# A fused linear-attention and expert kernel: the opening's loads reordered, three tiles transposed on TensorE, and the norm issued two tiles ahead

## The chip, the cores and the metric

The kernel runs on one core of one Trainium2 chip. The metric is the device time of one launch in microseconds, as the median of repeated runs. A core has five engines that work side by side and meet through semaphores: TensorE (PE in the profile, with weight loads shown apart as PEld), VectorE (DVE), ScalarE (ACT), GpSimd (POOL) and SyncE (SP), which only issues transfers. Each engine executes its instructions strictly in the order in which the program gives them.

## The reference

A sequence of 2048 tokens with 640 columns is normalised, and the sum of three things is returned: the input, a linear attention over the normalised input, and an expert layer that adds its own input and changes eight tokens of it.

```python
xn = layernorm(x)                                  # over 640 columns
# A: linear attention, 32 heads of 20 columns
q, k, v = split(xn @ wqkv)
phi = lambda t: where(t > 0, t + 1, exp(t)) + 1e-6
kv = einsum("bhsd,bhse->bhde", phi(k), v)
z = einsum("bhsd->bhd", phi(k))
o = einsum("bhqd,bhde->bhqe", phi(q), kv) / (einsum("bhqd,bhd->bhq", phi(q), z)[..., None] + 1e-6)
A = o @ wo
# B: one expert for the 8 tokens with the largest r
r = xn @ w_r
idx = argsort(-r)[:8]
y = (silu(xn[idx] @ w_gate) * (xn[idx] @ w_up)) @ w_down * sigmoid(r[idx])
B = xn, with y added to the rows idx
return x + A + B
```

## The kernel before

The tokens are cut into 16 tiles of 128. All of x, its normalised form `xn`, the transposed `xnT`, phi of q (transposed, `pqT`) and phi of k (`pk`) stay in SBUF.

**The main loop** (lines 365 to 398) takes one tile per iteration. TensorE makes k of the tile (`k_mm`, line 240, ten products, whose last column is the router's r), then a part of the product of `xn` and `pk` of the tile before (`ga_mm`, line 263, three products; `pk` of the tile before is its operand), then q (`q_mm`, line 252, 25 products with the weights `wq` as the stationary operand). ScalarE makes exp and relu of k and q (`phi_act`, lines 220 and 223) and copies the router column to `r_all` (line 384). VectorE joins exp and relu to `pk` and `pqT` (`phi_vec`, line 232).

**The layer norm** of a tile is made ahead of the loop's use of it. `ln_stats` runs two statistics instructions (line 161) and joins them (line 165) on VectorE; then come four small steps on columns of one element: add epsilon (169), a power for the root (174), a second power for the reciprocal (176), and a copy of the mean (177). They run on GpSimd, apart from the first tiles (those below `LN_FAST`), where VectorE copies the mean and takes the reciprocal. `ln_norm` (line 189) then writes `xn` on VectorE. From tile `PE_TR` on a DMA transpose, issued by SP (line 194), writes `xnT`; the tiles below are transposed on TensorE (`tr_tile`, line 199) and copied from PSUM (`tr_evict`).

The order on each engine is that of the program text (the tile framework is in manual schedule). In iteration t VectorE does: the statistics of tile t + 4, `pqT` of tile t - 1, the norm of tile t + 3, `pk` of tile t; from iteration 12 also residual additions (line 354). Small constants on GpSimd (`small_consts`) and the later loads on SP (`late_loads`, line 337) follow at the end of an iteration.

**The opening** (lines 100 to 111) issues the first loads from two queues, SP and ACT: x tile 0 in two halves, the k weights `wk` on ACT in two parts around x tiles 1 and 2 on SP, then the q weights `wq` and x tile 3 on SP, and x tiles 4 to 7 on ACT. Meanwhile TensorE runs `WARM` = 13 products of zeros (line 273). The router weights `wrow` are transposed by TensorE and copied into the last column of `wk` (line 284).

**After the loop** come the choice of the eight tokens, the sums over the tokens, the expert, the denominators, the per-head products, and an output loop (line 689) over the 16 tiles.

Of the kernel before, what the change touches and what calls it, by code (L numbers as in the profile page):

```python
# [8 lines left out]
P = 128  # L9
S = 2048  # L10
D = 640
# [3 lines left out]
T = S // P  # L15
KC = D // P
FC = F // P
C = 8
TBLK = 512
# [4 lines left out]
EB = 80  # L24
NEB = D // EB
EPS_BF16 = 1.0013580322265625e-05
PE_TR = 2
LN_FAST = 3
WARM = 13
LASTW = 448  # L30
AHEAD = 4

BF16 = mybir.dt.bfloat16
# [10 lines left out]
def kernel(  # L44
# [13 lines left out]
    nc = tc.nc  # L58
# [4 lines left out]
    x_v = A_x[0].rearrange("(t p) d -> p t d", p=P)  # L63
    out_v = out[0].rearrange("(t p) d -> p t d", p=P)
    wqkv_v = A_wqkv.rearrange("(kc p) n -> p kc n", p=P)
# [6 lines left out]
    def sb(shape, dt, name, tag=None):  # L72
        return big.tile(shape, dt, tag=tag or name, name=name)

    def pair(tag, name):
        return psum.tile([P, 2 * TBLK], F32, tag=tag, name=name)

    def bank(tag, name):
        return psum.tile([P, TBLK], F32, tag=tag, name=name)

    x_sb = sb([P, T, D], BF16, "x_sb")
    xn = sb([P, T, D], BF16, "xn")
    xnT = sb([P, KC, S], BF16, "xnT")
    pqT = sb([P, KC, S], BF16, "pqT")
    pk = sb([P, T, D], BF16, "pk")
    wk = sb([P, KC, D + 1], BF16, "wk")
    wq = sb([P, KC, D], BF16, "wq")
    wv = sb([P, KC, D], BF16, "wv")
# [12 lines left out]
    nc.gpsimd.dma_start(wrow[:], B_w_r.rearrange("(kc p) -> kc p", p=P))  # L101
    nc.sync.dma_start(x_sb[:, 0, 0:HW], x_v[:, 0, 0:HW])
    nc.scalar.dma_start(x_sb[:, 0, HW:D], x_v[:, 0, HW:D])
    nc.scalar.dma_start(wk[:, 0:2, 0:D], wqkv_v[:, 0:2, D : 2 * D])
    for t in (1, 2):
        nc.sync.dma_start(x_sb[:, t, :], x_v[:, t, :])
    nc.scalar.dma_start(wk[:, 2:KC, 0:D], wqkv_v[:, 2:KC, D : 2 * D])
    nc.sync.dma_start(wq[:, 0:3, :], wqkv_v[:, 0:3, 0:D])
    nc.sync.dma_start(wq[:, 3:KC, :], wqkv_v[:, 3:KC, 0:D])
    nc.sync.dma_start(x_sb[:, 3, :], x_v[:, 3, :])  # L110
    nc.scalar.dma_start(x_sb[:, 4:8, :], x_v[:, 4:8, :])


    zero = sb([P, TBLK], BF16, "zero")
# [43 lines left out]
    def ln_half(t, h):  # L158
        if h == 0:
            stat[t] = work.tile([P, 2, nc.vector.BN_STATS_DIM], F32, tag="stats", name=f"st{t}")  # L160
        nc.vector.bn_stats(out=stat[t][:, h, :], in_=x_sb[:, t, h * HW : (h + 1) * HW])  # L161

    def ln_aggr(t):
        mv = work.tile([P, 2], BF16, tag="mv", name=f"mv{t}", bufs=4)
        nc.vector.bn_aggr(out=mv[:], in_=stat[t][:])  # L165
        sc = work.tile([P, 2], F32, tag="sc", name=f"sc{t}", bufs=4)
        sq = work.tile([P, 2], BF16, tag="sq", name=f"sq{t}", bufs=4)
        scal[t] = sc, sq
        (nc.vector if t == 0 else nc.gpsimd).tensor_scalar(  # L169
            out=sq[:, 0:1], in0=mv[:, 1:2], scalar1=EPS_BF16, scalar2=None, op0=ALU.add  # L170
        )
        if t < LN_FAST:
            nc.vector.tensor_copy(sc[:, 0:1], mv[:, 0:1])  # L173
        nc.gpsimd.tensor_tensor(out=sq[:, 1:2], in0=sq[:, 0:1], in1=half[:], op=ALU.pow)  # L174
        if t >= LN_FAST:
            nc.gpsimd.tensor_tensor(out=sc[:, 1:2], in0=sq[:, 1:2], in1=neg1[:], op=ALU.pow)  # L176
            nc.gpsimd.tensor_copy(sc[:, 0:1], mv[:, 0:1])  # L177

    def ln_stats(t):
        ln_half(t, 0)  # L180
        ln_half(t, 1)
        ln_aggr(t)

    def ln_norm(t):
        sc, sq = scal[t]
        if t < LN_FAST:
            nc.vector.reciprocal(sc[:, 1:2], sq[:, 1:2])
        for a, b in ((0, 2 * P), (2 * P, D)) if t == 0 else ((0, D),):
            nc.vector.tensor_scalar(  # L189
                out=xn[:, t, a:b], in0=x_sb[:, t, a:b], scalar1=sc[:, 0:1], scalar2=sc[:, 1:2],  # L190
                op0=ALU.subtract, op1=ALU.mult,
            )
        if t >= PE_TR:
            nc.sync.dma_start_transpose(xnT[:, :, t * P : (t + 1) * P], xn[:, t, :])

    def tr_tile(t):
        ptr = bank("D1", f"tr{t}").bitcast(BF16)
        for kc in range(KC):
            nc.tensor.transpose(
                ptr[:, kc * P : (kc + 1) * P], xn[:, t, kc * P : (kc + 1) * P], ident[:]  # L200
            )
        return ptr

    def tr_evict(t, ptr):
        src = ptr[:, 0:D].rearrange("p (k f) -> p k f", k=KC)
        dst = xnT[:, :, t * P : (t + 1) * P]
        if t == 0:
            nc.scalar.copy(dst[:, 0:2, :], src[:, 0:2, :])
            nc.scalar.copy(dst[:, 2:KC, :], src[:, 2:KC, :])
        elif t == 1:  # L210
            nc.vector.tensor_copy(dst, src)
        else:
            nc.scalar.copy(dst, src)

    r_all = sb([P, T], BF16, "r_all")

# [18 lines left out]

    def k_mm(t):
        ps = pair("A", f"k{t}")
        for kc in range(KC):
            for a, b in ((0, TBLK), (TBLK, D + 1)):
                nc.tensor.matmul(  # L240
                    ps[:, a:b],
                    lhsT=xnT[:, kc, t * P : (t + 1) * P],
                    rhs=wk[:, kc, a:b],
                    start=(kc == 0), stop=(kc == KC - 1),
                )
        return ps

    def q_mm(t):
        ps = pair("B", f"q{t}")
        for m in range(KC):  # L250
            for kc in range(KC):
                nc.tensor.matmul(  # L252
                    ps[:, m * P : (m + 1) * P],
                    lhsT=wq[:, kc, m::KC],
                    rhs=xnT[:, kc, t * P : (t + 1) * P],
                    start=(kc == 0 and m in (0, 4)), stop=(kc == KC - 1),
                    skip_group_check=True,
                )
        return ps
# [11 lines left out]
    warm = pair("B", "warm")  # L271
    for i in range(WARM):
        nc.tensor.matmul(warm[:, 0:TBLK], lhsT=zero[:, 0:P], rhs=zero[:], start=True, stop=True)
# [4 lines left out]
    pg = bank("D0", "pg").bitcast(BF16)  # L278
    nc.tensor.transpose(pg[:, 0:P], headg[:].rearrange("p j h -> p (j h)"), ident[:])
    nc.scalar.copy(grep[:], pg[:, 0:P])  # L280
    tr_evict(0, tr_tile(0))
    prep = bank("D0", "prep").bitcast(BF16)
    nc.tensor.transpose(prep[:, 0:KC], wrow[:], ident[0:KC, 0:KC])
    nc.scalar.copy(wk[:, :, D], prep[:, 0:KC])  # L284
    ln_stats(1)
    ln_stats(2)
    ln_norm(1)
    ln_stats(3)

    iof = sb([P, 32], F32, "iof")  # L290
    boff = sb([NTB, 1], F32, "boff")
# [43 lines left out]
    def late_loads(t):  # L335
        def part(dst, src, a, b):
            nc.sync.dma_start(dst[:, a:b, :], src[:, a:b, :])

        wv_v = wqkv_v[:, :, 2 * D : 3 * D]
        plan = {  # L340
            0: (x_sb, x_v, 8, 12), 1: (wv, wv_v, 0, 3), 2: (wv, wv_v, 3, KC),
            3: (x_sb, x_v, 12, 16), 4: (wo, wo_v, 0, 4), 5: (wo, wo_v, 4, 8),
            6: (wg, kcF, 0, 2), 7: (wg, kcF, 2, 4), 8: (wg, kcF, 4, 5),
            9: (wu, kcU, 0, 2), 10: (wu, kcU, 2, 4), 11: (wu, kcU, 4, 5),
            12: (wd, kcD, 0, 6), 13: (wd, kcD, 6, 12),
        }
        if t in plan:
            part(*plan[t])
# [15 lines left out]

    for t in range(T):
        kp = k_mm(t)
        if t == 0:
            tr_evict(1, tr_tile(1))
        else:
            ga_mm(t - 1)  # L370
        qp = q_mm(t)
        if t == 0:
            ln_norm(2)
        else:
            if t == 1:
                q_phi(t - 1, qer)
            if t + 4 < T:
                ln_stats(t + 4)
            if t > 1:
                q_phi(t - 1, qer)  # L380
            if t + 3 < T:
                ln_norm(t + 3)
        ker = phi_act(kp, "k")
        nc.scalar.copy(r_all[:, t : t + 1], kp[:, D : D + 1])
        if t > 12:
            residual(4 * (t - 13) + 3)
        phi_vec(pk[:, t, :], ker, False)
        if t == 0:
            ln_norm(3)
            ln_stats(4)  # L390
        qer = phi_act(qp, "q")
        if t > 11:
            for u in range(4 * (t - 12), 4 * (t - 12) + 3):
                residual(u)
        small_consts(t)
        late_loads(t)
        if t > 12:
            keep(4 * (t - 13), 4 * (t - 12))
# [31 lines left out]
    for t in range(T):  # L430
        i = t % 4
        for a, b in ((0, TBLK), (TBLK, D)):
            nc.tensor.matmul(
                zp[32 * i : 32 * i + 32, a:b],
                lhsT=ones_bf[:],
                rhs=pk[:, t, a:b],
                start=(t < 4), stop=(t >= T - 4),
# [23 lines left out]
    for t in range(6):  # L461
# [4 lines left out]
        start=True, stop=True,  # L466
# [59 lines left out]
    for m in range(KC):  # L526
        for j in range(NTB):
            nc.tensor.matmul(  # L528
                pden[32 * j : 32 * j + 32, :],
                lhsT=zm[:, m, :],  # L530
                rhs=pqT[:, m, j * TBLK : (j + 1) * TBLK],
                start=(m == 0), stop=(m == KC - 1),
# [12 lines left out]
    for a, w in enumerate((wg, wu)):  # L545
        for kc in range(KC):
            for j in range(4):
                nc.tensor.matmul(  # L548
                    gu[32 * j : 32 * j + 32, a * TBLK : a * TBLK + FJ],
                    lhsT=xsT[:, kc, :],  # L550
                    rhs=w[:, kc, j * FJ : (j + 1) * FJ],
                    start=(kc == 0), stop=(kc == KC - 1),
# [59 lines left out]
    for fc in range(FC):  # L612
        j, b = fc // 3, fc % 3
        for i in range(4):
            nc.tensor.matmul(
                py[32 * i : 32 * i + 32, 0:QW],
                lhsT=hT[:, 4 * b + j, :],
                rhs=wd[:, fc, i * QW : (i + 1) * QW],
                start=(fc == 0), stop=(fc == FC - 1),
# [53 lines left out]
    for m in range(KC):  # L673
        pm = pair("ACBAC"[m], f"M{m}")
        for a, b in ((0, TBLK), (TBLK, D)):
            for i in range(2):
                for g in range(4):
                    nc.tensor.matmul(  # L678
                        pm[32 * g : 32 * g + 32, a:b],
                        lhsT=kvT[:, 2 * g + i, m, :],  # L680
                        rhs=wo[:, 2 * g + i, a:b],
                        start=(i == 0), stop=(i == 1),
# [67 lines left out]
```

## Time and profile before

| what | value |
|---|---|
| median of 3 runs | 118.1 us (117.92 to 119.11) |
| the profiled execution's own time | 119.11 us |
| its span, first to last instruction | 117.4 us |
| TensorE busy | 108.2 us, 92% of the span |
| VectorE busy | 85.7 us, 73% |
| ScalarE busy | 57.0 us, 49% |
| GpSimd busy | 38.3 us, 33% |
| chain that ended last, by engine | TensorE 69%, DMA 12%, VectorE 5%, GpSimd 3%, ScalarE 3% |
| mean granted TensorE clock | 0.982 |

The profile is of one execution. Busy shares are averages over the whole span, and stages differ: the opening, the loop, the part behind it and the output loop each have their own limit. The chain that ended last is followed back from the last instruction, at each step to what released it. Idle time of an engine is put down to the instruction or transfer whose end came last. L240 means line 240 of the kernel.

### The profile page before, as it was taken

To read this page: it belongs to the slowest core of one execution; us is meant where nothing else is said; L and a number is where in the kernel's file an instruction comes from. 1 tells how busy PE (TensorE), PEld (TensorE's weight loads), DVE (VectorE), ACT (ScalarE), POOL (GpSimd) and SP (SyncE) were. 2 spreads that over 40 slices of the span, in tenths; PEclk is the share of its full clock that TensorE was granted. 3 is DMA by queue.
4 is the path that set the end of the run, shared out by engine and by line. 5 is a ranking of instruction groups with operands and counts; after the bars stand their busy time and mean duration, and the time that the engine had idled before them with its cause. 6 is when DMAs were issued, how large, how long until landed. Compare 5 with 4: busy or idle time off the path is not lost.

```text
span 117.4 us, 2966 instructions
## 1 busy us (share of the span) xinstructions
PE 108.2 (92%) x1166; PEld 72.1 (61%) x1178; DVE 85.7 (73%) x193; ACT 57.0 (49%) x103; POOL 38.3 (33%) x88
## 2 busy tenths in 40 slices
PE   5976995999999999999999999989999999999980
PEld 2334972777667777766777754436896655555540
DVE  6681778998888988885999998810778466655570
ACT  4031488278877777887777790049622700000000
POOL 5332348779878677553000000040053000000000
PEclk9998699999999999999999999999999999999998
DMA  3996049996999999899799990600002599963333
GB/s 77 331 377 216 4 85 72 296 273 124 228 184 212 288 266 176 200 267 272 204 265 362 388 335 7 225 6 0 0 6 20 133 332 284 378 223 114 112 112 112
DMA packets 24814, 22.20 MB, mean 189 GB/s; under 512 B 11104, under 2 KB 23520, under 8 KB 24800
## 3 DMA queue, kind: packets, MB, share of 16 engines
q1 hardware_dynamic: 21840, 19.21, 63.1%
q10 hardware_dynamic: 2784, 2.76, 6.8%
q0 software_dynamic: 176, 0.04, 0.5%
q8 instruction: 9, 0.15, 0.5%
q14 instruction: 5, 0.04, 0.2%
HBM read 14.42 MB, written 5.28 MB: 168 GB/s over the span
## 4 chain that ended last, share of the span: by engine, by line
PE 69%; DMA 12%; DVE 5%; POOL 3%; ACT 3%; SPq 2%; issue 2%; ACTq 0%; DVEq 0%
PE o L689 18%; PE q L252 17%; PE k L240 15%; DMA x_sb<-in_A_x_dram 8%; PE gaC L263 5%; DMA zrel<-zpart 5%; PE gbC L565 4%; PE gaD L263 3%; PE M L678 2%; DVE st L161 1%; PE gu L548 1%; POOL sc L176 1%; PE pden L528 1%; POOL sq L174 1%; PE pkv L642 1%
## 5 line engine op out<-in xcount | busy, mean ns | idle before, releaser
L252 PEld LDWEIGHTS <-wq 128*128 128x128 bf16 x400 | 25.5, 119 | 3.2
L240 PE MATMUL k<-wk,xnT 128*128 128x129 bf16 (+1 forms) x152 | 24.7, 298 | 2.2 <-ACT wk L284 1.4
L252 PE MATMUL q<-xnT,wq 128*128 128x128 bf16 x400 | 26.1, 224 | 0.0
L689 PE MATMUL o<-M,pqT 128*128 128x128 bf16 (+2 forms) x152 | 21.3, 299 | 0.2
L697 DVE TENSOR_TENSOR o_t<-o,x_sb 128x640 bf16<-128x640 f32 (+1 forms) x16 | 13.0, 813 | 9.1 <-PE o L689 9.0
L240 PEld LDWEIGHTS <-xnT 128*128 128x128 bf16 x160 | 12.5, 98 | 9.7 <-issue 1.7
L689 PEld LDWEIGHTS <-pqT 128*128 128x128 bf16 x160 | 12.4, 98 | 9.4
L220 ACT ACTIVATE eq<-q 128x640 bf16<-128x640 f32 x16 | 11.3, 704 | 13.6 <-PE q L252 13.6
L161 DVE BATCH_NORM_STATS2 st<-x_sb 128x6 f32<-128x320 bf16 x32 | 14.1, 482 | 3.4 <-DMA x_sb<-in_A_x_dram 3.4
L232 DVE SCALAR_TENSOR_TENSOR pqT<-eq,rq 128x640 bf16<-128x640 bf16 x16 | 13.0, 814 | 2.7 <-ACT rq L223 2.7
L232 DVE SCALAR_TENSOR_TENSOR pk<-ek,rk 128x640 bf16<-128x640 bf16 x16 | 13.2, 823 | 2.1 <-ACT rk L223 1.9
L174 POOL TENSOR_TENSOR sq<-sq,half 128x1 bf16<-128x1 bf16 x16 | 12.8, 798 | 2.4 <-DVE sc L173 1.1
L220 ACT ACTIVATE ek<-k 128x640 bf16<-128x640 f32 x16 | 11.3, 705 | 2.9 <-PE k L240 1.7
L223 ACT ACTIVATE rq<-q 128x640 bf16<-128x640 f32 x16 | 11.2, 698 | 0.0
L223 ACT ACTIVATE rk<-k 128x640 bf16<-128x640 f32 x16 | 11.2, 697 | 0.0
L263 PE MATMUL gaC<-pk,xn 128*128 128x512 bf16 x32 | 9.5, 377 | 1.6 <-DVE pk L232 1.6
L169 POOL TENSOR_SCALAR sq<-mv 128x1 bf16<-128x1 bf16 x15 | 5.0, 331 | 14.2 <-DVE mv L165 14.2
L497 POOL COPY xsT<-xnT 128x5 bf16 x8 | 1.2, 222 | 23.3 <-DMA zrel<-zpart 23.3
L176 POOL TENSOR_TENSOR sc<-sq,neg 128x1 f32<-128x1 bf16 x13 | 8.1, 624 | 1.0
L189 DVE TENSOR_SCALAR xn<-x_sb,sc 128x640 bf16<-128x640 bf16 (+2 forms) x17 | 7.3, 433 | 1.2 <-POOL sc L177 1.1
L263 PEld LDWEIGHTS <-xn 128*128 128x128 bf16 x48 | 4.1, 97 | 5.5 <-issue 1.8
L454 PE MATMUL gbA<-pk,xn 128*128 128x512 bf16 x31 | 7.2, 380 | 0.1
(127 smaller groups left out, 111.0 us busy)
## 6 DMA issues: line engine op xcount, KB each, us to landing
xcp<-x_sb SPq DMA_DIRECT2D x4, 640.0 KB, 5.8
wd<-in_B_w_down_dram SPq DMA_DIRECT2D x2, 960.0 KB, 6.7
x_sb<-xcp SPq DMA_DIRECT2D x3, 640.0 KB, 7.3
wg<-in_B_w_gate_dram SPq DMA_DIRECT2D x2, 768.0 KB, 5.5
wu<-in_B_w_up_dram SPq DMA_DIRECT2D x2, 768.0 KB, 5.7
x_sb<-in_A_x_dram SPq DMA_DIRECT2D x2, 640.0 KB, 5.8
out_dram<-o_t SPq DMA_DIRECT2D x8, 160.0 KB, 2.4
out_dram<-o_t ACTq DMA_DIRECT2D x7, 160.0 KB, 1.9
```

The lines of the kernel that those rows point to most:

```text
L161: nc.vector.bn_stats(out=stat[t][:, h, :], in_=x_sb[:, t, h * HW : (h + 1) * HW])
L174: nc.gpsimd.tensor_tensor(out=sq[:, 1:2], in0=sq[:, 0:1], in1=half[:], op=ALU.pow)
L176: nc.gpsimd.tensor_tensor(out=sc[:, 1:2], in0=sq[:, 1:2], in1=neg1[:], op=ALU.pow)
L189: nc.vector.tensor_scalar(out=xn[:, t, a:b], in0=x_sb[:, t, a:b], scalar1=sc[:, 0:1], scalar2=sc[:, 1:2], op0=ALU.subtract, op1=ALU.mult,)
L220: nc.scalar.activation(e[:], ps[:, 0:D], AF.Exp)
L223: nc.scalar.activation(r[:], ps[:, 0:D], AF.Relu)
L232: nc.vector.scalar_tensor_tensor(out=dst, in0=ea, scalar=1.0, in1=ra, op0=ALU.min, op1=ALU.add)
L240: nc.tensor.matmul(ps[:, a:b], lhsT=xnT[:, kc, t * P : (t + 1) * P], rhs=wk[:, kc, a:b], start=(kc == 0), stop=(kc == KC - 1),)
L252: nc.tensor.matmul(ps[:, m * P : (m + 1) * P], lhsT=wq[:, kc, m::KC], rhs=xnT[:, kc, t * P : (t + 1) * P], start=(kc == 0 and m in (0, 4)) ...
L263: nc.tensor.matmul(gaC[:, c * TBLK : (c + 1) * TBLK] if c < 2 else gaD[:], lhsT=xn[:, t, c * P : (c + 1) * P], rhs=pk[:, t, 0:TBLK], start ...
L689: nc.tensor.matmul(po[:, a + o : b + o], lhsT=pqT[:, m, t * P : (t + 1) * P], rhs=M[:, m, a:b], start=(m == 0), stop=(m == KC - 1),)
L697: nc.vector.tensor_tensor(out=o_t[:, a:b], in0=po[:, a + o : b + o], in1=x_sb[:, t, a:b], op=ALU.add)
```

## The change

The change does these things:

- The loads of the opening are in another order: the k weights right behind x tile 0 (first part on SP, second on ACT), then x tiles 1, 2 and 3 on SP, the q weights split over both queues, x tiles 4 to 7 last on SP. Of the later loads, the first two are exchanged: part of the v weights is issued in iteration 0, x tiles 8 to 11 in iteration 1.
- Nine zero products instead of 13.
- Tile 0 is transposed in two parts, each with its own PSUM tile and its own copy.
- k of tile 0 first makes all products of columns 0 to 511, and then all products of the last 129 columns, the router's among them.
- q of tile 0 is made in two parts, with the transposes of tile 1 between them.
- Tile 2 is transposed on TensorE in iteration 1 and copied by ScalarE, instead of by DMA.
- Tile 2 takes its reciprocal on GpSimd (`LN_FAST` 2).
- In iteration t VectorE does the norm of tile t + 2 first, then the statistics of tile t + 3, `pqT` of tile t - 1 and `pk` of tile t.

```diff
-PE_TR = 2
-LN_FAST = 3
-WARM = 13
+PE_TR = 3
+LN_FAST = 2
+WARM = 9
...
-    nc.scalar.dma_start(wk[:, 0:2, 0:D], wqkv_v[:, 0:2, D : 2 * D])
-    for t in (1, 2):
+    nc.sync.dma_start(wk[:, 0:2, 0:D], wqkv_v[:, 0:2, D : 2 * D])
+    nc.scalar.dma_start(wk[:, 2:KC, 0:D], wqkv_v[:, 2:KC, D : 2 * D])
+    for t in (1, 2, 3):
         nc.sync.dma_start(x_sb[:, t, :], x_v[:, t, :])
-    nc.scalar.dma_start(wk[:, 2:KC, 0:D], wqkv_v[:, 2:KC, D : 2 * D])
-    nc.sync.dma_start(wq[:, 0:3, :], wqkv_v[:, 0:3, 0:D])
-    nc.sync.dma_start(wq[:, 3:KC, :], wqkv_v[:, 3:KC, 0:D])
-    nc.sync.dma_start(x_sb[:, 3, :], x_v[:, 3, :])
-    nc.scalar.dma_start(x_sb[:, 4:8, :], x_v[:, 4:8, :])
+    nc.scalar.dma_start(wq[:, 2:KC, :], wqkv_v[:, 2:KC, 0:D])
+    nc.sync.dma_start(wq[:, 0:2, :], wqkv_v[:, 0:2, 0:D])
+    nc.sync.dma_start(x_sb[:, 4:8, :], x_v[:, 4:8, :])
...
+        order = [(kc, c) for kc in range(KC) for c in ab]
+        if t == 0:
+            order = [(kc, c) for c in ab for kc in range(KC)]
...
-    tr_evict(0, tr_tile(0))
+    tra, trb = bank("D1", "tr0a").bitcast(BF16), pair("C", "tr0b").bitcast(BF16)
+    tr_tile(0, tra, 0, 2)
+    tr_evict(0, tra, 0, 2, nc.scalar.copy)
+    tr_tile(0, trb, 2, KC)
+    tr_evict(0, trb, 2, KC, nc.scalar.copy)
...
     ln_stats(1)
     ln_stats(2)
     ln_norm(1)
-    ln_stats(3)
...
-            0: (x_sb, x_v, 8, 12), 1: (wv, wv_v, 0, 3), 2: (wv, wv_v, 3, KC),
+            1: (x_sb, x_v, 8, 12), 0: (wv, wv_v, 0, 2), 2: (wv, wv_v, 2, KC),
...
     for t in range(T):
         kp = k_mm(t)
         if t == 0:
-            tr_evict(1, tr_tile(1))
+            qp = q_mm(t, None, range(0, 3))
+            tr1 = bank("D1", "tr1").bitcast(BF16)
+            tr_tile(1, tr1, 0, KC)
+            q_mm(t, qp, range(3, KC))
+            ln_half(3, 0)
+            tr_evict(1, tr1, 0, KC, nc.vector.tensor_copy)
+            ln_half(3, 1)
+            ln_aggr(3)
         else:
             ga_mm(t - 1)
-        qp = q_mm(t)
-        if t == 0:
-            ln_norm(2)
-        else:
+            if t == 1:
+                tr2 = bank("D1", "tr2").bitcast(BF16)
+                tr_tile(2, tr2, 0, KC)
+                tr_evict(2, tr2, 0, KC, nc.scalar.copy)
+            qp = q_mm(t)
+            if t + 2 < T:
+                ln_norm(t + 2)
             if t == 1:
                 q_phi(t - 1, qer)
-            if t + 4 < T:
-                ln_stats(t + 4)
+            if t + 3 < T:
+                ln_stats(t + 3)
             if t > 1:
                 q_phi(t - 1, qer)
-            if t + 3 < T:
-                ln_norm(t + 3)
         ker = phi_act(kp, "k")
...
         phi_vec(pk[:, t, :], ker, False)
         if t == 0:
-            ln_norm(3)
-            ln_stats(4)
+            ln_norm(2)
```

More of the change, by code (lines that the diff above doesn't have):

```diff
@@ L194, in ln_norm, with tr_tile @@
             nc.sync.dma_start_transpose(xnT[:, :, t * P : (t + 1) * P], xn[:, t, :])
-    def tr_tile(t):
-        ptr = bank("D1", f"tr{t}").bitcast(BF16)
-        for kc in range(KC):
+    def tr_tile(t, ptr, lo, hi):
+        for kc in range(lo, hi):
             nc.tensor.transpose(
@@ L201, in tr_tile, with tr_evict @@
             )
-        return ptr
-    def tr_evict(t, ptr):
+    def tr_evict(t, ptr, lo, hi, copy):
         src = ptr[:, 0:D].rearrange("p (k f) -> p k f", k=KC)
-        dst = xnT[:, :, t * P : (t + 1) * P]
-        if t == 0:
[L208 to L211, printed above, removed]
-        else:
-            nc.scalar.copy(dst, src)
+        copy(xnT[:, lo:hi, t * P : (t + 1) * P], src[:, lo:hi, :])
     r_all = sb([P, T], BF16, "r_all")
@@ L237, in k_mm, with q_mm @@
         ps = pair("A", f"k{t}")
[L238 to L245, printed above, removed]
-        return ps
-    def q_mm(t):
-        ps = pair("B", f"q{t}")
-        for m in range(KC):
+        ab = ((0, TBLK), (TBLK, D + 1))
+        order = [(kc, c) for kc in range(KC) for c in ab]
+        if t == 0:
+            order = [(kc, c) for c in ab for kc in range(KC)]
+        for kc, (a, b) in order:
+            nc.tensor.matmul(
+                ps[:, a:b],
+                lhsT=xnT[:, kc, t * P : (t + 1) * P],
+                rhs=wk[:, kc, a:b],
+                start=(kc == 0), stop=(kc == KC - 1),
+            )
+        return ps
+    def q_mm(t, ps=None, ms=range(KC)):
+        ps = ps or pair("B", f"q{t}")
+        for m in ms:
             for kc in range(KC):
@@ L367 @@
         if t == 0:
-            tr_evict(1, tr_tile(1))
+            qp = q_mm(t, None, range(0, 3))
[6 more added lines that the diff above has]
+            ln_aggr(3)
         else:
             ga_mm(t - 1)
-        qp = q_mm(t)
-        if t == 0:
-            ln_norm(2)
-        else:
+            if t == 1:
[5 more added lines that the diff above has]
+                ln_norm(t + 2)
             if t == 1:
                 q_phi(t - 1, qer)
-            if t + 4 < T:
-                ln_stats(t + 4)
+            if t + 3 < T:
+                ln_stats(t + 3)
             if t > 1:
                 q_phi(t - 1, qer)
-            if t + 3 < T:
-                ln_norm(t + 3)
         ker = phi_act(kp, "k")
```

## The prediction

> **What bounds the kernel now.** I read the table of busy time by stretch first, then the chain that ended last, then the timeline of a tile in the middle of the loop and of the first tiles. The table (stretch in us; busy us of each engine; granted clock, DMA share and GB/s at the end), and the chain (start, us, what):
>
> ```profile
> 7.90:20.50 12.60, 9.78 (x87) 7.26 (x89) 8.29 (x24) 7.16 (x16) 6.00 (x14) 0.86 0.56 115
> 26.00:40.00 14.00, 13.89 (x156) 10.14 (x156) 12.35 (x26) 10.67 (x21) 12.20 (x31) 1.00 1.04 200
> ...
> 11.00:12.00 1.00, 1.00 (x11) 1.00 (x10) 0.00 (x0) 0.65 (x2) 0.00 (x0) 0.50 0.09 32
> ```
>
> ```profile
> 2.20 0.44 SPq L108
> ...
> 2.67 0.49 SPq L109
> ...
> 3.21 9.03 DMA x_sb<-in_A_x_dram
> ...
> 20.57 0.59 PE gaC L263 x2
> ...
> 26.20 1.38 PE k L240 x10
> 27.58 0.43 PE gaC L263 x2
> 28.01 0.22 PE gaD L263
> 28.23 1.40 PE q L252 x25
> ...
> 65.92 1.41 PE q L252 x25
> 67.35 0.70 ACT eq L220
> ```
>
> In the middle TensorE is busy 13.89 of 14.00 us: a tile costs 1.38 + 0.43 + 0.22 + 1.40 = 3.43 us, and nothing else shows. But VectorE stands at 12.35 of 14.00, 88%, so it has little to give. Before 20.57 the loop isn't yet in this pace: the load of x tile 3 lands at 3.21 + 9.03 = 12.24, VectorE waits for it in its queue, and the chain runs through VectorE and GpSimd until the gate product of tile 1 starts at 20.57. So the most that the opening can give is the time by which that product comes earlier, and it counts only if the loop still runs at 3.43 afterwards. That is the question here. One tile from the timeline (start, us, engine, line, operation; the bracket is idle time):
>
> ```profile
> 29.70 0.87 DVE L161 BATCH_NORM_STATS2 st<-x_sb 128x6 f32<-128x320 bf16 x2
> 30.61 0.21 DVE L165 BATCH_NORM_AGGREGATE mv<-st 128x2 bf16<-128x12 f32 x1
> 30.90 0.23 POOL L169 TENSOR_SCALAR sq<-mv 128x1 bf16<-128x1 bf16 x1
> 30.99 0.83 DVE L232 SCALAR_TENSOR_TENSOR pqT<-eq,rq 128x640 bf16<-128x640 bf16 x1 [0.18 <-ACT rq L223]
> 31.21 1.03 POOL L174 TENSOR_TENSOR sq<-sq,half 128x1 bf16<-128x1 bf16 x1
> 31.73 0.44 DVE L189 TENSOR_SCALAR xn<-x_sb,sc 128x640 bf16<-128x640 bf16 x1
> ...
> 32.37 0.82 DVE L232 SCALAR_TENSOR_TENSOR pk<-ek,rk 128x640 bf16<-128x640 bf16 x1 [0.20 <-ACT rk L223]
> 32.83 0.41 POOL L177 CAST sc<-mv 128x1 f32<-128x1 bf16 x1
> ...
> 34.27 0.59 PE L263 MATMUL gaC<-pk,xn 128*128 128x512 bf16 x2
> ```
>
> The statistics end at 30.82 and GpSimd's four steps (add, power, power, copy) at 33.24: 2.42 us. Nobody waits for them, because the norm at 31.73 uses the steps of the tile before; its own come a whole iteration later.
>
> **A price for GpSimd beside VectorE.** The same steps in the first tiles, where the norm did wait for them:
>
> ```profile
> 13.18 0.21 DVE L165 BATCH_NORM_AGGREGATE mv<-st 128x2 bf16<-128x12 f32 x1
> 14.21 0.82 DVE L232 SCALAR_TENSOR_TENSOR pk<-ek,rk 128x640 bf16<-128x640 bf16 x1
> 14.44 1.00 POOL L176 TENSOR_TENSOR sc<-sq,neg 128x1 f32<-128x1 bf16 x1
> 15.62 0.45 DVE L189 TENSOR_SCALAR xn<-x_sb,sc 128x640 bf16<-128x640 bf16 x1 [0.59 <-POOL sc L177]
> 15.98 0.88 DVE L161 BATCH_NORM_STATS2 st<-x_sb 128x6 f32<-128x320 bf16 x2
> 16.89 0.21 DVE L165 BATCH_NORM_AGGREGATE mv<-st 128x2 bf16<-128x12 f32 x1
> 17.02 0.77 DVE L232 SCALAR_TENSOR_TENSOR pqT<-eq,rq 128x640 bf16<-128x640 bf16 x1
> 17.19 0.68 POOL L169 TENSOR_SCALAR sq<-mv 128x1 bf16<-128x1 bf16 x1 [1.61 <-DVE mv L165]
> 17.71 0.88 DVE L161 BATCH_NORM_STATS2 st<-x_sb 128x6 f32<-128x320 bf16 x2
> 17.96 0.57 POOL L174 TENSOR_TENSOR sq<-sq,half 128x1 bf16<-128x1 bf16 x1
> 18.61 0.55 POOL L176 TENSOR_TENSOR sc<-sq,neg 128x1 f32<-128x1 bf16 x1
> ...
> 19.33 0.45 DVE L189 TENSOR_SCALAR xn<-x_sb,sc 128x640 bf16<-128x640 bf16 x1 [0.50 <-POOL sc L177]
> ```
>
> An add that starts inside pqT (17.19) takes 0.68 instead of 0.23 and ends at 17.87, 0.08 after pqT's end at 17.79. A power that starts inside pk (14.44) ends at 15.44, 0.41 after pk's end at 15.03; the one at 31.21, inside pqT, ends at 32.24, 0.42 after 31.82. Those that start beside the statistics (17.96, 18.61) take 0.57 and 0.55. So a GpSimd step that begins while VectorE runs a two-input operation is held to that operation's end: an add then ends 0.08 after it, a power 0.42 after it. From the end of the statistics to the norm it took 15.62 - 13.39 = 2.23 us, and 19.33 - 17.10 = 2.23 us, both with one such stop.
>
> The Trainium skill, page "SBUF — State Buffer", on the shared port pair, says that VectorE and GpSimd take a lock on a pair of ports and that the loser blocks fully; an operation with two SBUF inputs takes it. Going by it, a stopped power would run its whole 0.57 after the release, a tile would cost 0.15 more than below, and the forecast would rise by about 1.6 us; the three rows above end at 0.41 and 0.42, so the sum goes by them.
>
> **The change part by part.** *Norm two tiles ahead.* In iteration t VectorE's order was statistics(t+4), pqT(t-1), norm(t+3), pk(t). It becomes norm(t+2), statistics(t+3), pqT(t-1), pk(t). No operation is added, but a loop closes: norm(t+2) stands ahead of statistics(t+3), these ahead of GpSimd's steps, and these ahead of norm(t+3). With a norm at 0, from the rows: statistics at 0.36 (15.62 to 15.98), their end at 1.48 (17.10); pqT starts at 1.40 (17.02), pk at 2.09 (as the statistics at 17.71 did behind pqT) and ends at 2.91. The add is held to 2.25; the power starts at 2.34, inside pk, and ends at 2.91 + 0.42 = 3.33; the second power 3.41 to 3.96, the copy to 4.11, the next norm at **4.15 us**. That is 0.72 over TensorE's 3.43, and VectorE idles 1.24 of it. With one stop it would be 1.48 + 2.23 = 3.71. To stay hidden the steps must take 3.43 - 1.48 = 1.95 from the end of the statistics.
>
> Would pqT and pk come later, and let the steps through? At TensorE's pace pk ends at 33.19 and the gate product starts at 34.27, so VectorE may fall 1.08 behind before TensorE notices. Once behind, rq and rk are there before VectorE asks, pqT and pk follow the statistics at once, and both stops happen each tile. Behind the waiting norm stand all of VectorE's work and, through pk, TensorE's next gate product. Eleven rounds lead from norm(4) to norm(15). The last is longer: three residual additions (below, 1.28) and three small operations stand ahead of norm(15): 2.91 - 0.08 + 1.28 + about 0.5, say 4.65.
>
> ```profile
> 57.10 1.28 DVE L354 TENSOR_TENSOR x_sb<-x_sb,xn 128x640 bf16<-128x640 bf16 x3
> ```
>
> After norm(15) VectorE has only pqT, pk and residuals, per iteration 0.69 + 0.82 - 0.08 + 4 x 0.43, about 3.2: pk(15) ends at 0.36 + 0.74 + 0.43 + 0.82 + 2 x 3.2 = 8.75 after it, and the gate product of tile 15 starts at 8.8. TensorE is there at about 8. Before, that product followed q of tile 15 (65.92 + 1.41 = 67.33) and pk(15); call it 67.5.
>
> *Loads.* The k weights move ahead of x tiles 1 and 2, the q weights behind x tile 3 on SP and second on ACT; x tiles 4 to 7 go from ACT to SP's end, and the first v weights follow them at once, as SP has no transpose to wait for in iteration 0. The bytes ahead of q's weights stay much the same.
>
> ```profile
> 1.25 5.73 PE L273 MATMUL warm<-zero 128*128 128x512 bf16 x13 [1.25 <-DVE zero L115]
> ...
> 11.11 0.74 PE L199 MATMUL tr<-ident,xn 128*128 128x128 bf16 x5
> ...
> 11.64 2.61 PE L252 MATMUL q<-xnT,wq 128*128 128x128 bf16 x23
> ```
>
> ```profile
> wq<-in_A_wqkv_dram SPq DMA_DIRECT2D x1, 480.0 KB, 7.6
> ...
> wq<-in_A_wqkv_dram SPq DMA_DIRECT2D x1, 320.0 KB, 8.7
> ```
>
> Their second part (line 109) landed at 2.67 + 8.7 = 11.4. By the rows the new landing lies between 9.8 (the first part, 2.20 + 7.6) and 12.24 (x tile 3, last on SP); I take 10.8, near 11.4 with some credit for the split over two queues.
>
> *Zero products, router column, transposes of tiles 0 and 1.* Four zero products fewer, 4 x 5.73 / 13 = 1.8 us, the two-part transpose and the router column last bring k of tile 0 forward by about 2 us; the wait for q's weights hides all of it (if they came at 9.8, up to 1 us of it would show). q of tile 0 stops after 15 products; tile 1's transposes follow. At the half clock of the row at 11.00 a q product takes 2.61 / 23 = 0.113: tile 1 is transposed at 10.8 + 1.7 + 0.74 = 13.2, copied from 13.3. VectorE, in order: half of the statistics of tile 3 to 14.4, pk(0), norm(2) at 15.0, norm(3) 2.3 after the statistics at 16.7, pqT(0), statistics(4) to 18.9.
>
> *Tile 2 on TensorE.* Five transposes, and one copy on ACT that I set at 0.7 like its other passes over 640 columns, ahead of ek(1). TensorE: rest of q(0) to 14.3, k(1) to 15.7, gate product to 16.4, transposes to about 16.9; ACT: copy to 17.7, ek and rk to 19.2. The DMA transpose that goes from SP was nobody's wait in these rows. pk(1) ends at 20.1, the gate product of tile 1 starts there, against 20.57: a gain of about 0.4. norm(4) follows GpSimd at about 21.1.
>
> *Sum.* norm(15) at 21.1 + 10 x 4.15 + 4.65 = 67.25, the last gate product at 76.05, against 67.5: **+8.5 us**. What follows the loop keeps its order and length. The profiled execution took 119.11 with a span of 117.4, so 127.6 by its own time; the median of the runs, 118.1, lies 1.0 below it, and I forecast **126.6**. The bounds of q's weights, 9.8 and 12.24, move this to 125.6 and 128.0.
>
> **Rivals.** *One stop a tile* (3.71): for it, both measured waits had one; against it, pqT and pk now both stand behind the statistics. Ten rounds save 4.4: 122.2. *Steps hidden, faster:* if GpSimd gets through in 1.95, TensorE's pace of 3.43 holds from the gate product of tile 1; that product comes at 20.1, or at 18.7 with q's weights at 9.8 and 0.4 for a full clock: 116.2 to 117.6. Against it: no wait in the rows was under 2.23. *Clock:* in each round TensorE idles 0.72 of 4.15. Work at the half clock of the row at 11.00 would be 6.86 a tile; if every second round ran so, the average would be (4.15 + 6.86) / 2 = 5.5, eleven times 1.35 more: 141. The Trainium skill, page "TensorE: Matmul & The Clock Gate", section on the second HAM failure mode, tells of short idles that throttle again. The row 7.90:20.50, busy 9.78 of 12.60, 78%, has 0.86, and the loop would be 83% busy, so it can't be excluded. *The loads don't come sooner* (12.24): 128.0, in the forecast's own range.
>
> **From cases to numbers.** Two stops 0.73, one stop 0.12, hidden 0.08, clock 0.03, something between that ends within 1% 0.04. Forecast 126.6, alone 125 to 128.5; with the one-stop case the range is 121.5 to 128.5. About 1% is what a measurement of this kernel can tell from no change: faster 0.08, same 0.04, slower 0.88.
>
> **What would show it.** Right: norms from tile 4 on preceded by VectorE idle of about 1.2 us, released by GpSimd's copy; 4.1 to 4.2 us from gate product to gate product, TensorE idle 0.7 before each, released by pk; first powers of 0.9 to 1.0. Wrong: a period of 3.43 with norms that don't wait, or powers of 0.57 in the middle of the loop.

## The result and the profile after

The changed kernel takes 125.76 us (median of 5 runs, 125.13 to 127.59) against 118.1 us: 1.060 times as long, interval 1.056 to 1.065. It is slower by 7.7 us. The profiled execution, the slowest of the five, took 127.59 us with a span of 125.9 and had a lower TensorE clock in the opening (0.73 in the first row below), so its times from there on are some 1.8 us late against the median; the ratios in this document leave out such slow runs, the medians do not.

The same two stretches as before, from the table of busy time by stretch, and below them the two waits on which the reading rests (waiter, for whom: us in total, times, longest):

```profile
7.90:20.50 12.60, 10.49 (x92) 7.66 (x91) 7.80 (x21) 5.92 (x12) 5.71 (x12) 0.73 0.42 123
26.00:40.00 14.00, 12.35 (x133) 8.65 (x131) 10.16 (x23) 8.99 (x17) 9.61 (x24) 1.00 0.80 158
```

```profile
DVE xn L188 <- POOL sc L176: 15.1, 12, 1.5
...
PE gaC L256 <- DVE pk L222: 6.8, 13, 0.6
```

In the middle of the loop TensorE is now busy 12.35 of 14.00 us instead of 13.89, and VectorE 10.16 instead of 12.35. Both have become less busy, at a full clock (1.00) and with less traffic (158 GB/s against 200): neither is held up by the amount of its own work. The norm waits twelve times for GpSimd's copy, 15.1 us in all; in the kernel before it waited twice, 1.1 us. One round of the loop, from one norm to the next, in the timeline:

```profile
25.48 0.45 DVE L188 TENSOR_SCALAR xn<-x_sb,sc 128x640 bf16<-128x640 bf16 x1 [1.23 <-POOL sc L176]
25.84 0.88 DVE L160 BATCH_NORM_STATS2 st<-x_sb 128x6 f32<-128x320 bf16 x2
...
26.76 0.21 DVE L164 BATCH_NORM_AGGREGATE mv<-st 128x2 bf16<-128x12 f32 x1
26.88 0.77 DVE L222 SCALAR_TENSOR_TENSOR pqT<-eq,rq 128x640 bf16<-128x640 bf16 x1
27.06 0.68 POOL L168 TENSOR_SCALAR sq<-mv 128x1 bf16<-128x1 bf16 x1 [1.61 <-DVE mv L164]
...
27.57 0.82 DVE L222 SCALAR_TENSOR_TENSOR pk<-ek,rk 128x640 bf16<-128x640 bf16 x1
...
27.82 1.00 POOL L173 TENSOR_TENSOR sq<-sq,half 128x1 bf16<-128x1 bf16 x1
...
28.44 0.59 PE L256 MATMUL gaC<-pk,xn 128*128 128x512 bf16 x2 [0.55 <-DVE pk L222]
...
28.90 0.55 POOL L175 TENSOR_TENSOR sc<-sq,neg 128x1 f32<-128x1 bf16 x1
...
29.40 0.18 POOL L176 CAST sc<-mv 128x1 f32<-128x1 bf16 x1
...
29.62 0.45 DVE L188 TENSOR_SCALAR xn<-x_sb,sc 128x640 bf16<-128x640 bf16 x1 [1.23 <-POOL sc L176]
```

Follow one line of descent here: norm, statistics, add, power, power, copy, norm. It takes 29.62 - 25.48 = 4.14 us. The add starts inside pqT and ends 0.09 after it (27.74 against 27.65); the power starts inside pk and ends 0.43 after pk's end (28.82 against 28.39). VectorE stands idle 1.23 us, and 13 of the 16 gate products wait for pk, this one 0.55 us. The chain that ended last has changed hands accordingly. Below are its shares by engine, and then its pieces at the first products of q and at the last gate product:

```profile
PE 34%; DVE 27%; POOL 22%; DMA 9%; issue 4%; SPq 2%; DVEq 0%; ACT 0%; POOLq 0%
```

```profile
3.17 7.68 DMA wq<-in_A_wqkv_dram
10.90 1.82 PE q L245 x15
...
75.11 0.75 DVE pk L222
75.89 0.59 PE gaC L256 x2
```

TensorE's share fell from 69% to 34%; VectorE and GpSimd, 8% together before, now hold 49%.

### The profile page after: what moved, and what is told of

It is laid out like the page before. It is cut to its first block, busy times and chain, and to the rows that moved or that the text cites. A ratio compares the mean times of both kernels' runs of the same rounds, so it can differ in the third digit from the quotient of the medians.

```text
span 125.9 us, 2978 instructions
## 1 busy us (share of the span) xinstructions
PE 110.4 (88%) x1179; PEld 72.3 (57%) x1179; DVE 84.0 (67%) x191; ACT 57.7 (46%) x104; POOL 42.0 (33%) x90
## 4 chain that ended last, share of the span: by engine, by line
PE 34%; DVE 27%; POOL 22%; DMA 9%; issue 4%; SPq 2%; DVEq 0%; ACT 0%; POOLq 0%
PE o L692 17%; POOL sq L173 9%; DVE st L160 8%; POOL sq L168 7%; DMA wq<-in_A_wqkv_dram 6%; POOL sc L175 5%; DVE xn L188 5%; PE gbC L568 4%; DVE x_sb L350 4%; DVE pqT L222 3%; DMA zrel<-zpart 3%; DVE pk L222 2%; PE M L681 2%; DVE mv L164 2%; PE gbA L457 2%
## 5 line engine op out<-in xcount | busy, mean ns | idle before, releaser
L233 PE MATMUL k<-wk,xnT 128*128 128x512 bf16 (+1 forms) x160 | 25.9, 308 | 1.1 <-ACT r_all L388 0.6
L692 PE MATMUL o<-M,pqT 128*128 128x512 bf16 (+2 forms) x155 | 21.5, 301 | 0.0
L233 PEld LDWEIGHTS <-xnT 128*128 128x128 bf16 x160 | 13.1, 101 | 9.7 <-issue 2.5
L188 DVE TENSOR_SCALAR xn<-x_sb,sc 128x640 bf16<-128x640 bf16 (+2 forms) x17 | 7.4, 441 | 15.2 <-POOL sc L176 15.1
L168 POOL TENSOR_SCALAR sq<-mv 128x1 bf16<-128x1 bf16 x15 | 9.5, 635 | 23.9 <-DVE mv L164 23.6
L173 POOL TENSOR_TENSOR sq<-sq,half 128x1 bf16<-128x1 bf16 x16 | 13.9, 868 | 2.2 <-DVE sc L172 1.0
L222 DVE SCALAR_TENSOR_TENSOR pqT<-eq,rq 128x640 bf16<-128x640 bf16 x16 | 12.6, 787 | 0.0
```

The source lines that it names most:

```text
L168: (nc.vector if t == 0 else nc.gpsimd).tensor_scalar(out=sq[:, 0:1], in0=mv[:, 1:2], scalar1=EPS_BF16, scalar2=None, op0=ALU.add)
L188: nc.vector.tensor_scalar(out=xn[:, t, a:b], in0=x_sb[:, t, a:b], scalar1=sc[:, 0:1], scalar2=sc[:, 1:2], op0=ALU.subtract, op1=ALU.mult,)
L222: nc.vector.scalar_tensor_tensor(out=dst, in0=ea, scalar=1.0, in1=ra, op0=ALU.min, op1=ALU.add)
L233: nc.tensor.matmul(ps[:, a:b], lhsT=xnT[:, kc, t * P : (t + 1) * P], rhs=wk[:, kc, a:b], start=(kc == 0), stop=(kc == KC - 1),)
L692: nc.tensor.matmul(po[:, a + o : b + o], lhsT=pqT[:, m, t * P : (t + 1) * P], rhs=M[:, m, a:b], start=(m == 0), stop=(m == KC - 1),)
```

## The experiments

The theory is that of the prediction: the round norm, statistics, GpSimd's four steps, norm is what costs. The rivals put the loss on the opening, on the number of stops, or on the distance of two tiles as such. In the diffs a minus stands for the changed kernel and a plus for the experiment, unless said otherwise; the runs of the kernel before that went with them gave 118.12 us (first four, on one chip) and 118.42 us (last four, on another).

### The new opening with the old order in the loop

```diff
-            if t + 2 < T:
-                ln_norm(t + 2)
             if t == 1:
+                ln_norm(3)
                 q_phi(t - 1, qer)
-            if t + 3 < T:
-                ln_stats(t + 3)
+            if t + 4 < T:
+                ln_stats(t + 4)
             if t > 1:
                 q_phi(t - 1, qer)
+            if t + 3 < T:
+                ln_norm(t + 3)
...
         if t == 0:
             ln_norm(2)
+            ln_stats(4)
```

> The changed kernel with the order of before on VectorE in the loop: the norm three tiles ahead, the statistics four. Loads, zero products and transposes stay as changed. Theory (the loss is the round norm, statistics, GpSimd's steps, norm): 3.43 us from gate product to gate product, no norm that waits in the middle of the loop, the gate product of tile 1 at about 20.1, 117.6 us (116.5 to 118.2). Rival (the new opening or its transposes cost the time): 124 us or more, whatever the order in the loop.

116.8 us, ratio to before 0.9925 (0.9876 to 0.9974). Its middle stretch and its only piece of the chain at the gate product of tile 1:

```profile
26.00:40.00 14.00, 13.88 (x160) 10.25 (x160) 12.36 (x26) 10.90 (x21) 11.22 (x28) 1.00 1.08 216
```

```profile
18.18 0.38 PE gaC L256
```

TensorE is back at 13.88 of 14.00. From 21.60 on the gate products are 3.43 apart, and from norm(4) on no norm waits. So the opening doesn't cost anything; it gains 1.3 us by the medians and 0.9 by the ratio, whose interval runs from 0.3 to 1.5. The gate product of tile 1 starts at 18.18 instead of the forecast's 20.1. Here q's weights were there at 9.85 and the clock of the first stretch was 1.00; with these two the forecast's own working gives 18.7, and the other 0.5 was not traced.

### The old opening with the new order in the loop

The minus here stands for the kernel before.

```diff
-            if t == 1:
-                q_phi(t - 1, qer)
-            if t + 4 < T:
-                ln_stats(t + 4)
-            if t > 1:
-                q_phi(t - 1, qer)
-            if t + 3 < T:
-                ln_norm(t + 3)
+            if t + 2 < T:
+                ln_norm(t + 2)
+            if t == 1:
+                q_phi(t - 1, qer)
+            if t + 3 < T:
+                ln_stats(t + 3)
+            if t > 1:
+                q_phi(t - 1, qer)
...
-        if t == 0:
-            ln_norm(3)
-            ln_stats(4)
```

> The kernel before with nothing but the norm two tiles ahead. Theory: the loss is there without anything of the new opening: 4.14 us a tile from norm(4), which comes at about 20.1, to norm(15) at about 66.0, the last gate product at about 74.6, 125.2 us (124 to 126.5). Rival (the opening is needed for the loss): 117 to 119 us.

125.06 us, ratio 1.060 (1.050 to 1.071): the whole loss, with nothing of the new opening. Its norms from tile 4 to tile 14 stand 4.14 apart (once 4.22), each with a wait for GpSimd:

```profile
19.26 0.45 DVE L189 TENSOR_SCALAR xn<-x_sb,sc 128x640 bf16<-128x640 bf16 x1 [1.54 <-POOL sc L177]
...
23.40 0.45 DVE L189 TENSOR_SCALAR xn<-x_sb,sc 128x640 bf16<-128x640 bf16 x1 [1.23 <-POOL sc L177]
...
27.54 0.45 DVE L189 TENSOR_SCALAR xn<-x_sb,sc 128x640 bf16<-128x640 bf16 x1 [1.23 <-POOL sc L177]
```

The two experiments together separate the change: the order in the loop costs about 7 us with the old opening and 9 with the new one (125.76 - 116.8), and the opening gains only where the loop can use it. Under the new order it gains nothing that shows (125.76 against 125.06), since the rounds start from norm(4), and that waits for GpSimd in either opening (at 19.26 here, and at 18.92 with the new opening in the next experiment).

### pqT ahead of the statistics: one stop instead of two

```diff
             if t + 2 < T:
                 ln_norm(t + 2)
-            if t == 1:
-                q_phi(t - 1, qer)
+            q_phi(t - 1, qer)
             if t + 3 < T:
                 ln_stats(t + 3)
-            if t > 1:
-                q_phi(t - 1, qer)
```

> The changed kernel with pqT of the tile before ahead of the statistics, so that behind the statistics stands only pk. One stop of GpSimd's steps a tile instead of two. Theory (what counts is the whole way from norm to norm): norm 0.36, pqT 0.69, statistics 1.12, then 2.23 with one stop: 4.40 us a tile, some 0.26 more than now, about 128.3 us. Rival (the number of stops alone sets the loss): about 3.7 us a tile, 121 to 122.5 us.

128.61 us. One round of it:

```profile
36.72 0.45 DVE L188 TENSOR_SCALAR xn<-x_sb,sc 128x640 bf16<-128x640 bf16 x1 [1.54 <-POOL sc L176]
...
38.73 0.21 DVE L164 BATCH_NORM_AGGREGATE mv<-st 128x2 bf16<-128x12 f32 x1
...
39.03 0.68 POOL L168 TENSOR_SCALAR sq<-mv 128x1 bf16<-128x1 bf16 x1 [1.09 <-DVE mv L164]
...
39.79 0.57 POOL L173 TENSOR_TENSOR sq<-sq,half 128x1 bf16<-128x1 bf16 x1
...
41.16 0.53 DVE L188 TENSOR_SCALAR xn<-x_sb,sc 128x640 bf16<-128x640 bf16 x1 [1.54 <-POOL sc L176]
```

The add is stopped by pk, the power runs its free 0.57, and from the end of the statistics (38.94) to the norm it takes 2.22, the one-stop figure of the prediction. Still the round takes 4.44 and the kernel is slower. The stops are a part of the price; what sets the time is the length of the whole round, and pqT now lies on it.

### One power instead of two

```diff
+    neghalf = sb([P, 1], F32, "neghalf")
+    nc.vector.memset(neghalf[:], -0.5)
...
+        if t < LN_FAST:
             nc.gpsimd.tensor_tensor(out=sq[:, 1:2], in0=sq[:, 0:1], in1=half[:], op=ALU.pow)
-        if t >= LN_FAST:
-            nc.gpsimd.tensor_tensor(out=sc[:, 1:2], in0=sq[:, 1:2], in1=neg1[:], op=ALU.pow)
+        else:
+            nc.gpsimd.tensor_tensor(out=sc[:, 1:2], in0=sq[:, 0:1], in1=neghalf[:], op=ALU.pow)
```

> The changed kernel with one power to the minus one half in place of the two powers from tile 2 on. It leaves out the rounding of the root to bf16 between them. Theory: the add and the power are stopped as before, power's end at 3.33 in the round, copy to 3.48, norm at 3.52: 3.52 us a tile instead of 4.14, 11 rounds, 6.8 us less, about 119 us. Rival (VectorE's or ScalarE's own work sets the 4.14): no difference, 125.8 us.

117.82 us, ratio 1.000 (0.997 to 1.003). Shortening GpSimd's steps by one power takes 7.9 us from the kernel, so VectorE's and ScalarE's own work is not the limit. Two norms, two gate products and a late k of it:

```profile
28.27 0.45 DVE L191 TENSOR_SCALAR xn<-x_sb,sc 128x640 bf16<-128x640 bf16 x1 [0.60 <-POOL sc L179]
...
31.77 0.45 DVE L191 TENSOR_SCALAR xn<-x_sb,sc 128x640 bf16<-128x640 bf16 x1 [0.60 <-POOL sc L179]
```

```profile
45.34 0.59 PE L259 MATMUL gaC<-pk,xn 128*128 128x512 bf16 x2
...
48.85 0.59 PE L259 MATMUL gaC<-pk,xn 128*128 128x512 bf16 x2
...
55.37 1.56 PE L236 MATMUL k<-wk,xnT 128*128 128x512 bf16 x10 [0.81 <-DMA xnT<-xn]
```

The round is 3.50, 0.07 over TensorE's pace, and it still sets the pace: up to 27.75 the gate products are 3.43 apart, and from there to 52.35 they follow at 3.51 on average, each 0.05 to 0.12 behind pk's end. Then k of one tile waits 0.81 us for its transpose, whose transfer took 5.45 us from issue to landing. From the gate product of tile 1 to that of tile 15 it takes 48.56 us here (17.46 to 66.02), against 46.95 in the first experiment (18.18 to 65.13). My 119 us was 1.2 too high, in part because it counted only the rounds from norm(4) on. The norms of tiles 3 and 4 come sooner as well: from norm(2) to norm(4) it takes 5.00 us here (12.75 to 17.75), against 6.12 in the third experiment (12.80 to 18.92), which has the same opening. The rest was not traced.

### The norm behind the statistics, still two tiles ahead

```diff
-            if t + 2 < T:
-                ln_norm(t + 2)
-            if t == 1:
-                q_phi(t - 1, qer)
             if t + 3 < T:
                 ln_stats(t + 3)
-            if t > 1:
-                q_phi(t - 1, qer)
+            if t + 2 < T:
+                ln_norm(t + 2)
+            q_phi(t - 1, qer)
```

> The changed kernel, norm still two tiles ahead, but behind the statistics of tile t + 3 instead of ahead of them. Theory (what costs is that nothing but pqT and pk stands between a tile's statistics and its norm): GpSimd now also has the next statistics, 1.12 us, to hide behind; its steps end before the norm is due, VectorE doesn't wait in the middle of the loop, 3.43 us a tile, 116 to 117.5 us. Rival (two tiles ahead is too near in itself): 4.1 us a tile, 125 us.

116.23 us, ratio 0.9825 (0.9789 to 0.9862): faster than both kernels, and the lowest median of this study, though the seventh experiment on the same chip lies within 0.3 of it. One tile of it:

```profile
30.05 0.87 DVE L160 BATCH_NORM_STATS2 st<-x_sb 128x6 f32<-128x320 bf16 x2
...
31.08 0.39 DVE L188 TENSOR_SCALAR xn<-x_sb,sc 128x640 bf16<-128x640 bf16 x1
31.25 0.30 POOL L168 TENSOR_SCALAR sq<-mv 128x1 bf16<-128x1 bf16 x1 [0.43 <-DVE mv L164]
31.28 0.59 PE L256 MATMUL gaC<-pk,xn 128*128 128x512 bf16 x2
...
31.64 1.00 POOL L173 TENSOR_TENSOR sq<-sq,half 128x1 bf16<-128x1 bf16 x1
...
32.81 0.83 DVE L222 SCALAR_TENSOR_TENSOR pk<-ek,rk 128x640 bf16<-128x640 bf16 x1 [0.61 <-ACT rk L213]
33.21 0.47 POOL L176 CAST sc<-mv 128x1 f32<-128x1 bf16 x1
...
34.71 0.59 PE L256 MATMUL gaC<-pk,xn 128*128 128x512 bf16 x2
```

The power is stopped as in the changed kernel (1.00), the copy too (0.47 and an end at 33.68). But the norm that needs it comes behind the next statistics, so nobody waits; the gate products are 3.43 apart, and from norm(4) to norm(14) VectorE's only waits are for ScalarE. The distance of two tiles is not the fault. Moving the norm from ahead of the statistics to behind them is worth 9.5 us (the edit also moves pqT(0) behind the statistics of tile 4, in iteration 1 alone).

### Parts of the opening

The next three start from the first experiment's kernel, and the minus stands for it. The loads in the order of before (the first two of the later loads too):

```diff
-    nc.sync.dma_start(wk[:, 0:2, 0:D], wqkv_v[:, 0:2, D : 2 * D])
-    nc.scalar.dma_start(wk[:, 2:KC, 0:D], wqkv_v[:, 2:KC, D : 2 * D])
-    for t in (1, 2, 3):
+    nc.scalar.dma_start(wk[:, 0:2, 0:D], wqkv_v[:, 0:2, D : 2 * D])
+    for t in (1, 2):
...
+    nc.scalar.dma_start(wk[:, 2:KC, 0:D], wqkv_v[:, 2:KC, D : 2 * D])
+    nc.sync.dma_start(wq[:, 0:3, :], wqkv_v[:, 0:3, 0:D])
...
```

> The first experiment's kernel (new opening, old order in the loop) with the loads of the opening in the order of before. Theory (the order of the loads is what the opening gains by): q's weights land about 1.2 us later, and all behind them moves, 117.9 us against 116.8. Rival (the transposes and the split of q gain it): 116.8 us.

13 zero products:

```diff
-WARM = 9
+WARM = 13
```

> The first experiment's kernel with 13 zero products instead of 9. Theory: k of tile 0 starts about 1 us later, inside the wait for q's weights (1.8 us in the first experiment): no difference, 116.8 us, within 0.3. Rival (the zero products were on the path): 117.8 us.

Tile 2 transposed by DMA:

```diff
-PE_TR = 3
+PE_TR = 2
...
-            if t == 1:
-                tr2 = bank("D1", "tr2").bitcast(BF16)
-                tr_tile(2, tr2, 0, KC)
-                tr_evict(2, tr2, 0, KC, nc.scalar.copy)
```

> The first experiment's kernel with tile 2 transposed by DMA instead of TensorE. Without the copy of 0.69 us on ScalarE, ek and rk of tile 1 come earlier; against it the transpose has to land before k of tile 2 at about 16.5, and the norm of tile 2 ends at 13.6. Theory (the two cancel): 116.4 to 117.2 us. Rival (the TensorE transposes of tile 2 are the opening's gain): 118 us.

The old loads gave 117.26 us (ratio 0.989, 0.985 to 0.993), 13 zero products 116.53 us (0.984, 0.981 to 0.987), tile 2 by DMA 119.22 us (1.004, 0.997 to 1.011). TensorE's longest wait in the opening of each, in this order:

```profile
PE k L234 <- DMA wk<-in_A_wqkv_dram: 2.1, 1, 2.1
```

```profile
PE q L245 <- DMA wq<-in_A_wqkv_dram: 1.7, 1, 1.7
```

```profile
PE k L233 <- DMA xnT<-xn: 2.5, 1, 2.5
```

Zero products make no difference: they lie inside the wait for q's weights (116.53 against 116.8, though on another chip). The order of the loads is worth 0.6 to 0.7 us (117.26 against 116.53, on one chip; the two intervals just overlap, so the size stays open), with the wait moving from k's weights to q's; that lies between my theory and the rival. The transposes of tile 2 on TensorE are the opening's larger gain, and here I was wrong by some 2 us: the DMA transpose was issued at 13.20 and landed 4.39 later, at 17.6, where I had assumed that it would be there at about 16.5. The wait was not the whole price, as this row shows:

```profile
17.64 2.86 PE L233 MATMUL k<-wk,xnT 128*128 128x512 bf16 x10 [2.49 <-DMA xnT<-xn]
```

Behind the wait the granted clock was 0.50 from 17.6 to 20.5, and k took 2.86 us, against 1.54 in the first experiment at 1.00.

## Why the prediction was right, point by point

The forecast was 126.6 us, and 125.76 was measured. **The round** was the step that decides, and it was right in size: 4.15 forecast, 4.14 measured, with two stops, VectorE idle 1.23 (1.24) and the power's end 0.43 after pk (0.42). TensorE idles 0.55 before a gate product and not 0.7, because the profile counts k to the end of its last product, 1.55 us against 1.38 in the chain's rows of before. In the profiled execution norm(4) started at 21.34 (21.1 forecast), norm(15) at 67.37 (67.25), the last gate product at 75.89 (76.05). The span grew by 125.9 - 117.4 = 8.5, the forecast's figure to the tenth.

```profile
21.34 0.45 DVE L188 TENSOR_SCALAR xn<-x_sb,sc 128x640 bf16<-128x640 bf16 x1 [1.54 <-POOL sc L176]
...
67.37 0.44 DVE L188 TENSOR_SCALAR xn<-x_sb,sc 128x640 bf16<-128x640 bf16 x1
```

That the profiled execution fits so well is partly luck. **The loads:** in it q's weights landed at 10.85 (10.8 forecast) and 15 products of q took 1.82, 0.121 each, at a granted clock of 0.50 (9.0 to 14.0), near the half clock on which the forecast had reckoned. In the experiments with this order of loads they landed at 9.5 to 9.9, around my lower bound of 9.8, and the clock from 9.0 to 14.0 was 1.00. The third experiment's program is the changed kernel's up to norm(4), and there norm(4) came so:

```profile
18.92 0.45 DVE L188 TENSOR_SCALAR xn<-x_sb,sc 128x640 bf16<-128x640 bf16 x1 [1.54 <-POOL sc L176]
```

That is 2.4 us sooner than in the profiled execution and 2.2 sooner than the forecast. Taken off the 127.59 us, it gives 125.2 as an estimate, at the low end of the other four runs (125.13 to 125.92). So the start of the rounds was the term that was too large, by about 2 us in those four runs if the estimate holds. The forecast missed the median by only 0.8, since 1.0 had been taken off for the profiled execution of before, whose clock was low too (0.86 in its first stretch).

**The price of a stopped step.** The Trainium skill, page "SBUF — State Buffer", section "SBUF: two separate sides", would have had a stopped power run whole after the release, as the prediction reads its full block. The rows say no: 27.82 + 1.00 = 28.82 is 0.43 after pk's end, not 0.57. In the sum the rows' price was the right one. (The prediction rests it on three rows; only two of them are powers, the third is an add.)

**A step that was missing.** I let k of tile 2 follow q of tile 1 at once. It waited 0.64 us:

```profile
19.04 1.54 PE L233 MATMUL k<-wk,xnT 128*128 128x512 bf16 x10 [0.64 <-ACT r_all L388]
```

k of every tile goes to the same PSUM tile, and is free only when ScalarE has copied the router column of the tile before. The new copy of tile 2's transposes stands in ScalarE's queue ahead of all that. I counted its 0.7 for pk(1), but not for this. The gate product of tile 1 came at 20.43 instead of 20.1, and nothing hung on it: norm(4) waited for GpSimd until 21.34.

**The opening's worth** was mis-sized too: 0.4 forecast. With a loop that can use it, it is 0.9 by the ratio of the first experiment (0.3 to 1.5) and 1.9 by that of the seventh (1.6 to 2.2), which differs only in the zero products and ran on another chip; how much of that lies in the chip stays open. I had taken the DMA transpose of tile 2 for "nobody's wait", from rows of before; the eighth experiment shows that in the faster opening it is a wait of 2.5 us. In the forecast this error had no weight, since norm(4) set the loop's start.

**The rivals.** One stop a tile did not come about. "Steps hidden" gave 116.2 to 117.6: the experiments that do hide them came out at 116.2 and 116.8. The clock stayed at 1.00 in the loop (26 to 40 us), with TensorE idle in each round. The loads landed at 10.85 and not at 12.24.

## What to carry to other kernels

When work is software-pipelined over two engines (started some tiles ahead of its use), don't count how many tiles ahead a step is issued; follow the value from its producer through the other engine back to its consumer, and see what the in-order engine has between them. If that is less work than the detour takes, the detour and everything in the loop ahead of the producer add up to a period of their own, and no engine need look fully busy (here TensorE 88% and VectorE 73% in the middle of the loop). Price the detour from rows in which it is disturbed by the same neighbours that it will have.

## What the runs showed of the hardware

GpSimd can hold up VectorE too, but here only a little. Where a mask was being made on GpSimd as the norm started, the norm took 0.53 instead of 0.45 (the norm at 41.16 in the third experiment's fence; the mask's step ran from 41.07 to 41.50). And the seventh transfer on SP, x tiles 4 to 7 (line 110), was issued only at 6.71, though the one before it was issued by 3.60. The wait in SP's queue in the changed kernel, as the profile puts it:

```profile
SPq L110 <- DMA wk<-in_A_wqkv_dram: 3.1, 1, 3.1
```

The program has no dependency of that load on k's weights; what held it, no run here tested. It delayed nothing: the load landed at 12.6, and the first statistics that read it started at 17.80.
